# Block-sorted attention and a squared-ReLU feed-forward in one kernel: fewer fp32 heads of q on SyncE, an earlier gate for the first x^T transposes, a new order of the first head pairs

## Chip, core and metric

One core of a Trainium2 chip runs the whole program. The metric is the time of one execution in microseconds (us), the median of several runs. Engine names as in the profile: PE is TensorE's matmuls, PEld its weight loads, DVE VectorE, ACT ScalarE, POOL GpSimd, SP SyncE.

## What is computed

Attention over sorted blocks, then a feed-forward on its output. Batch 4, 8 heads, 768 positions of 64 elements, 8 blocks of 96 positions; the feed-forward takes 3072 tokens of 512 through 2048 hidden units.

```
P = sort_net                                  # [4, 8, 8, 8]
for _ in range(5):                            # Sinkhorn
    P = exp(P - max(P)); P /= sum(P, -1); P /= sum(P, -2)
k_s = einsum('bhij,bhjcd->bhicd', P, k_blocks)
v_s = einsum('bhij,bhjcd->bhicd', P, v_blocks)
o   = softmax(q_b @ k_s^T / sqrt(64)) @ v_s   # block by block
x   = o.transpose(0, 2, 1, 3).reshape(3072, 512)
out = relu(x @ w_in) ** 2 @ w_out             # fp32 [3072, 512]
```

## The kernel before

**Who sets the order.** The kernel does not issue instructions as it meets them. It adds operations to a `Plan`, each with an engine, a cost and what it depends on; `Plan.run` then writes out one fixed order for each engine. PE has two lists there, attention and feed-forward. A table `DUES` gives each attention step of the second half of batch 0 and of batches 1 to 3 a due place, counted in feed-forward chunks, and an attention step goes first when it is due and ready. The first half of batch 0 follows a string `FIRST` instead: K and V sort the block rows of a head pair (L620), S is scores and exponential (L691, L711), T turns the sorted V (L740), A is the product with V and its normalisation (L882, L892, L893), X turns the attention output into x^T (L941), F is a first piece of the up-projection (L968). A capital letter lets ACT copy out of PSUM, a small one DVE; the prime picks the PSUM buffer. The planner's costs are fixed numbers in the code; on the chip every engine works through its list in order.

**Opening.** SP loads `sort_net` and then q of heads 0 to 3 of batch 0 in fp32 into space of `xT` that is needed only later (`q32`, L313). POOL's queue casts while it loads (L324): q of heads 4 to 7 in two halves of 64 partitions, K and V of batch 0 in head pairs, four parts of `w_in`, four parts of `w_out`, and then batch 1: V, V, K, q, K, q, in halves of four heads. ACT and DVE do five Sinkhorn rounds (exponential L459, normalisations L402 to L406), and between the exponentials ACT casts q32 to bf16 (`cast`, L469) and copies the q transposes (L570) out of PSUM (L248). When the sorting matrix is ready (`p_ij`, L417), PE spreads it over the partitions (`p_spread`, L481) and DVE and POOL build the block weights `w_all` (L493).

Filler matmuls on `ones` (`fill`, L431) keep PE at work in the gaps that the plan foresees before the feed-forward starts; they are written into PE's list like everything else. In front of them stand trial instructions whose results nothing uses: four fp32 matmuls (L444), a product with a running sum and a reciprocal on DVE (L436 to L440), and an exponential with a scale from memory on ACT (L449).

**Rest.** From about 23 us on PE alternates between the second half of batch 0 and later batches' attention, and the feed-forward in units of 384 tokens: 64 up matmuls (L1010, ReLU on ACT L1018, square on DVE L1021), then 48 down matmuls (L1040). The second-half sorts of K and V are L656.

For batch 1 and later, sorted V (`vn`, L776) goes through DRAM to change its layout: SP writes `v_way` (L800), waits, and reads `vblk` (L806), which the product L882 needs. q of batch 1's first two pairs is transposed on PE (L570), the other pairs' K and q by the DMA crossbar.

x^T of the second half of batch 0 comes for its first three head pairs from crossbar transposes on SP (L917). The first of them is held back by a small copy on POOL, the gate (L923), that reads the third part of `w_out`, so that the transposes do not start before that part has landed. It is put in the plan where the first such transpose is made, and stands behind all loads of batch 1.

Of the kernel before, what the change touches and what calls it, by code (L numbers as in the profile page):

```python
# [18 lines left out]


DUES = {
    (0, "K"): (-232.0, -238.5, -413.0, -404.5),
    (0, "S"): (-204.0, -204.5, -355.5, -296.0),
    (0, "T"): (-231.5, -163.5, -378.0, -266.0),
    (0, "A"): (-198.0, -109.5, -291.0, -100.5),
    (0, "X"): (-51.5, -27.5, -263.5, -74.5),
    (0, "W"): (-288.5,),
    (1, "V"): (-107.5, -57.0),
    (1, "Q"): (-50.0,),
    (1, "N"): (None, -39.5),  # L30
    (1, "Z"): (None, None, 1.0, 47.5),
    (1, "S"): (-40.5, -15.5, 11.5, 49.5),
    (1, "A"): (-27.5, 2.5, 12.5, 51.5),
    (1, "X"): (22.0, 6.0, 42.5, 54.5),
    (2, "L"): (45.5,),
    (2, "N"): (70.5, 75.5),
    (2, "V"): (73.0, 79.0),
    (2, "Z"): (79.5, 85.0, 93.5, 93.0),
    (2, "S"): (80.0, 85.5, 99.5, 97.0),
    (2, "A"): (80.0, 87.5, 101.0, 98.5),  # L40
    (2, "X"): (89.5, 99.0, 125.0, 130.0),
    (3, "L"): (130.5,),
    (3, "N"): (130.5, 138.5),
    (3, "V"): (132.0, 143.0),
    (3, "Z"): (142.5, 143.0, 153.0, 145.0),
    (3, "S"): (148.0, 148.5, 161.0, 157.0),
    (3, "A"): (148.0, 156.5, 162.5, 157.5),
    (3, "X"): (155.5, 165.0, 169.0, 183.5),
}

FIRST = ("K0 v0 k1' S0 t0' v1 K2' k3 S1 A0 T1' V2' v3 S2 A1 T2' t3' S3 x0' A2 X1 F0 F1 A3 X2 F3 "
         "F4 x3 F6 F7")


class Op:
# [127 lines left out]
def kernel(  # L185
# [115 lines left out]
    for n in range(4):  # L301
# [5 lines left out]
    w_in_bf = const.tile([128, KC, d_ff], BF16)  # L307
    w_out_bf = const.tile([128, NT, d_model], BF16)
    xT = const.tile([128, KC, n_tok], BF16)
    q32 = [xT[:, 1 + g, 2 * S:].bitcast(FP32).rearrange("p (h x) -> p h x", h=2)  # L310
           for g in range(2)]
    for g in range(2):
        nc.sync.dma_start(out=q32[g], in_=q_r[0, :, 2 * g:2 * g + 2, :])  # L313
    w_all = const.tile([128, H + HP, NB, C0], BF16)
    w_t = const.tile([128, NH // 4, 4, NB], BF16)
    qkv = {}
# [35 lines left out]

    first = plan.add("DMA", 4.55, lambda e: None)
    landed["last"] = first
    load(0, 0, HP, HP, slice(0, 64))
    load(0, 0, HP, HP, slice(64, 128))
    id_op = plan.add("POOL", 0.4, lambda e: make_identity(nc, ident, nomemset=True))
    mask = const.tile([128, C0], BF16)
    mask_t = const.tile([128, 4], BF16)
# [21 lines left out]
    def loads_after(deps):  # L381
        for g in range(4):
            if g == 1:
                landed["last"] = plan.add("DMA", 0.4, lambda e: None, [landed["last"]])
            t = slice(NT // 4 * g, NT // 4 * (g + 1))
            dma(("w_out", g), 1.05, lambda t=t: (w_out_bf[:, t, :], w_out_r[:, t, :]), deps)
        for t, g in ((2, 0), (2, 1), (1, 0), (0, 0), (1, 1), (0, 1)):
            load(1, t, HP * g, HP, deps=deps)
            if t == 2 and g == 1:
                landed["last"] = plan.add("DMA", 1.5, lambda e: None, [landed["last"]])  # L390
# [36 lines left out]
    def fill(us, slot):  # L427
# [4 lines left out]
                out=p2[slot][:, 0, 0:128 * r].rearrange("p (r x) -> p r x", r=r), lhsT=ones,  # L432
                rhs=ones[:, None, :].to_broadcast([128, r, 128]), start=True, stop=True)

    t32 = xT[:, 3, 2 * S:].bitcast(FP32)
    nc.vector.memset(t32[:, 0:128], 1.0)  # L436
    nc.vector.scalar_tensor_tensor(
        out=t32[:, 128:136], in0=t32[:, 0:8], scalar=1.0, in1=t32[:, 8:16],
        op0=ALU.mult, op1=ALU.mult, accum_out=t32[:, 136:137])
    nc.vector.reciprocal(out=t32[:, 137:138], in_=t32[:, 136:137])  # L440

    def warm(e):
        for n in (8, 16):
            nc.tensor.matmul(out=p2[1][:, 0, 16 * n:17 * n], lhsT=t32[:, 0:128],  # L444
                             rhs=t32[:, 0:n], start=True, stop=True)
        fill(2.4, 0)

    def try_exp(e):
        nc.scalar.activation(out=t32[:, 140:148], in_=p2[1][:, 0, 128:136], func=AF.Exp,  # L449
                             scale=t32[:, 137:138])  # L450


    plan.add("PE", 4.3, warm, [plan.add("DVE", 1.1, lambda e: None)])
# [4 lines left out]
    for it in range(5):  # L458
        step = plan.add("ACT", 0.26, lambda e: nc.scalar.activation(  # L459
            out=p_sb, in_=p_sb, func=AF.Exp), [step])  # L460
        exps.append(step)
        if it == 0:
            plan.add("ACT", 0.4, try_exp, [step])
        if it == 1:
            plan.add("ACT", 0.6, make_sel, [step, id_op])
        if it in (1, 2):
            def cast(e, g=it - 1):
                alloc_qkv(0)
                nc.scalar.copy(out=qkv[0][0][:, 2 * g:2 * g + 2, :], in_=q32[g])  # L469

            casts.append(plan.add("ACT", 0.8, cast, [step, plan.add(
                "WAY", 2.6 + 0.9 * it, lambda e: None, tail=2.6 + 0.9 * it)]))
        step = plan.add("DVE", 0.66, lambda e: sink_norm(e, 0), [step])
        step = plan.add("DVE", 0.47 if it == 4 else 0.72, lambda e, it=it: sink_norm(e, 1, it == 4), [step])

# [81 lines left out]
    def s_q(b, hp, p0, p1, due=0, after=None, eng=AD):  # L557

        n = p1 - p0
        t = {}  # L560

        def mm(e):
            qb = qkv[b][0]
            if b == 0:
                t["p"] = psf.tile([128, NA, n], BF16, tag="pf", name="qtp")
            else:
                t["p"] = ps1.tile([128, NA, n], BF16, tag="p1", name="qtp")
            for a in range(NA):
                for h in range(2):
                    nc.tensor.transpose(  # L570
                        out=t["p"][64 * h:64 * (h + 1), a, :],
                        in_=qb[p0:p1, 2 * hp + h, D * a:D * (a + 1)],
                        identity=ident[p0:p1, p0:p1])
            if p0 == 0:
                tiles["qT", b, hp] = att.tile(
                    [128, NA, 128], BF16, tag="qT", name="qT", bufs=4)

        def ev(e):
            qT, src = tiles["qT", b, hp].rearrange("p a x -> p (a x)"), t["p"]
            if b == 0:  # L580
                copy(e, qT.rearrange("p (i c a) -> p i c a", a=NA, c=C0)
                     [:, p0 // C0:p1 // C0, :, :], src.rearrange("p a (i c) -> p i c a", c=C0))
            else:
                copy(e, qT.rearrange("p (i a c) -> p i a c", a=NA, c=C0)
                     [:, p0 // C0:p1 // C0, :, :], src.rearrange("p a (i c) -> p i a c", c=C0))

        if b == 0:
            dep = casts[hp] if hp < HP // 2 else landed[b, 0, HP, p0]
        else:
            dep = landed[b, 0, HP * (2 * hp // HP), 0]  # L590
        ring = rf if b == 0 else r1
        s1, old = ring.take()
        if p0 == 0:
            qTs[b, hp], oldq = rqT.take()
        else:
            oldq = []
        pe = plan.add("PE", 0.04 + 0.0023 * n, mm, [dep, id_op] + old, due, mode="col")
        readers[b].append(pe)
        op = one_of(eng, cost_b(NA * n), ev, [pe, after] + oldq)
        ring.use(s1, pe, op)  # L600
        rqT.use(qTs[b, hp], op)
        return op
# [309 lines left out]
    def s_xt(u, due=0, eng=AD, own=True):  # L912
        early = u.b == 0 and u.halves == (1,) and u.hp < HP - 1
        if early or u.b > 1 or u.b == 1 and u.hp < HP - 1:
            def turn(e):
                t0 = S * u.b + BLK * u.i0
                nc.sync.dma_start_transpose(  # L917
                    out=xT[:, u.hp, t0:t0 + BLK * u.ni].rearrange("p (n q) -> p n q", q=BLK),
                    in_=u.ao.rearrange("p n e d -> p (n e d)"))

            if early and "gate" not in holds:
                def gate(e):
                    nc.gpsimd.tensor_copy(out=xT[0:1, 0:HP - 1, HS:HS + 1],  # L923
                                          in_=w_out_bf[0:1, 3 * NT // 4 - HP + 1:3 * NT // 4, 0:1])

                holds["gate"] = plan.add("POOL", 0.1, gate, [landed["w_out", 2]])
            sp = plan.add("SP", 1.4, turn, u.norms + [holds["gate"]] * early)
            op = plan.add("WAY", 6.0 if early else 1.3, lambda e: None, [sp], tail=3.8 if early else None)
            rao.use(u.nao, op)
            for hf in u.halves:  # L930
                x_done[u.b, u.hp, hf] = op
            return
# [46 lines left out]
    def put(key, t, n, dst, pe):  # L979

        st = {}
        so, old = rob.take()

        def cp(e):
            st["ob"] = ffn.tile([128, d_model], FP32, tag="ob", name="ob", bufs=4)
            copy(e, st["ob"][:, 0:n], t[key][:, 0:n])

        op = plan.add(AD, cost_f(n), cp, [pe] + old)
        sp = plan.add("SP", 0.55, lambda e: nc.sync.dma_start(out=dst, in_=st["ob"][:, 0:n]), [op])
        rob.use(so, plan.add("WAY", 1.5, lambda e: None, [sp], tail=0.9))  # L990
        return op

    def ffn_unit(g):
# [224 lines left out]
```

## Time and profile before

| | before |
|---|---|
| median of 3 runs | 219.79 us (219.42 to 220.04) |
| profiled execution | 219.84 us, span 218.1 us |
| PE busy | 209.6 us, 96% of the span |
| ACT, DVE, POOL busy | 121.9, 111.0, 28.3 us |
| DMA moved | 31.92 MB, mean 146 GB/s |
| granted TensorE clock, mean | 1.00 |

How to read the profile: a chain line gives start, length and what the time was spent on, followed back from the last instruction. A timeline line gives start, length, engine, line of the kernel, operation, out<-in and count. A wait line gives engine, what waited, what it waited for, us in total, times, and the longest. A queue line gives packets, MB, and the packets' time as a share of 16 DMA engines; q0 is the queue that POOL feeds, q1 SP's. "L882" is line 882 of the kernel it belongs to; the changed kernel is 18 lines shorter, so the same statement has a smaller number there.

### The profile page before, as it was taken

How to read it: one execution, taken by the hardware profiler on the slowest of the kernel's cores; microseconds unless marked ns; L12 is line 12 of the kernel's file. 1: busy time of each engine (PE TensorE's matmuls, PEld its weight loads, DVE VectorE, ACT ScalarE, POOL GpSimd, SP SyncE). 2: the span in 40 equal slices, each digit the busy share in tenths (PEclk: the TensorE clock that was granted, in tenths of full speed). 3: DMA queues.
4: the chain of work that ended last, by engine and by line, in shares of the span. 5: the costliest groups of instructions: out<-in, count | busy, mean ns of one | idle time of the engine just before them, and what ended most of it. 6: DMA issues, size and time to landing. Idle time of an engine off the chain costs nothing.

```text
span 218.1 us, 5074 instructions
## 1 busy us (share of the span) xinstructions
PE 209.6 (96%) x2024; PEld 116.3 (53%) x2041; DVE 111.0 (51%) x303; ACT 121.9 (56%) x250; POOL 28.3 (13%) x53
## 2 busy tenths in 40 slices
PE   6989999999899999999999999999999999999993
PEld 3457666446554555445665465445655455456552
DVE  6668586335696336653876045617685154015300
ACT  5767778228674457645784177327874375237421
POOL 7985221000000700000000420000000000000000
PEclk9999999999999999999999999999999999999999
DMA  6999999999986699299952699598985310120012
GB/s 152 199 189 207 207 206 212 181 152 278 259 164 59 142 203 227 57 170 252 185 171 52 134 182 221 108 196 185 153 203 116 88 45 3 48 96 0 3 57 89
DMA packets 47864, 31.92 MB, mean 146 GB/s; under 512 B 27296, under 2 KB 42912, under 8 KB 47840
## 3 DMA queue, kind: packets, MB, share of 16 engines
q0 software_dynamic: 12224, 13.24, 37.6%
q1 hardware_dynamic: 35616, 18.35, 37.6%
q8 instruction: 16, 0.26, 0.5%
q14 instruction: 8, 0.07, 0.1%
HBM read 29.70 MB, written 8.72 MB: 176 GB/s over the span
## 4 chain that ended last, share of the span: by engine, by line
PE 78%; DMA 11%; POOL 3%; DVE 3%; issue 1%; ACT 1%; POOLq 0%; DVEq 0%; SPq 0%
PE hp L1010 34%; PE op L1040 33%; DMA v_way<-vn 6%; DMA kb<-in_k_dram 3%; PE p L882 3%; PE p L691 3%; DMA vblk<-v_way 2%; PE op L1068 2%; PE p L776 1%; DVE ao L893 1%; POOL vb L324 1%; POOL kb L324 1%; PE p L656 1%; ACT h L1018 1%; DVE h L1021 1%
## 5 line engine op out<-in xcount | busy, mean ns | idle before, releaser
L1010 PE MATMUL hp<-xT,w_in_bf 128*128 128x384 bf16 x506 | 87.8, 326 | 0.0
L1040 PE MATMUL op<-w_out_bf,h 128*128 128x512 bf16 x351 | 83.4, 379 | 1.1 <-issue 0.3
L1018 ACT ACTIVATE h<-hp 128x384 bf16<-128x384 f32 x128 | 61.7, 495 | 19.5 <-PE hp L1010 16.5
L1021 DVE TENSOR_TENSOR h<-h 128x384 bf16<-128x384 bf16 x128 | 43.7, 355 | 49.1 <-ACT h L1018 48.6
L1010 PEld LDWEIGHTS <-w_in_bf 128*128 128x128 bf16 x506 | 47.5, 98 | 31.4 <-issue 0.5
L1040 PEld LDWEIGHTS <-h 128*128 128x128 bf16 x368 | 34.0, 98 | 38.4 <-issue 1.4
L248 ACT COPY ob<-op 128x512 f32<-128x512 f32 (+2 forms) x24 | 13.6, 568 | 47.1 <-PE op L1040 44.7
L720 ACT ACTIVATE et<-p 96x384 bf16<-96x384 f32 x48 | 19.7, 488 | 7.4 <-PE p L691 7.4
L893 DVE TENSOR_TENSOR ao<-p,rec 96x512 bf16<-96x512 f32 x32 | 22.0, 686 | 1.1
L882 PEld LDWEIGHTS <-et 96*128 96x128 bf16 x256 | 11.4, 97 | 5.3 <-DMA vblk<-v_way 0.9
L892 DVE RECIPROCAL rec<-p 96x8 f32<-96x8 f32 x32 | 6.4, 201 | 14.9 <-PE p L882 14.6
L1157 POOL COPY held<-xT 1x3 bf16<-1x3 bf16 (+1 forms) x2 | 0.4, 186 | 83.1 <-DMA xT<-ao 83.1
L882 PE MATMUL p<-vblk,et 96*128 96x65 bf16 x192 | 9.3, 193 | 0.6 <-DMA vblk<-v_way 0.6
L431 PE MATMUL p<-ones 128*128 128x512 bf16 (+1 forms) x29 | 9.2, 436 | 0.0
L691 PEld LDWEIGHTS <-kvT 64*128 64x128 bf16 x256 | 6.2, 94 | 5.5 <-issue 3.1
L250 DVE CAST vn<-p 128x768 bf16<-128x768 f32 x6 | 5.7, 958 | 6.1 <-PE p L776 6.0
L250 DVE CAST kn<-p 128x768 bf16<-128x768 f32 x5 | 4.8, 958 | 7.6 <-PE p L776 7.5
L836 DVE COPY kvT<-kx 128x768 bf16<-128x768 bf16 x10 | 8.5, 848 | 0.1
L248 ACT CAST vn<-p 128x768 bf16<-128x768 f32 x6 | 4.8, 801 | 5.4 <-PE p L776 5.4
L711 ACT ACTIVATE et<-p 96x768 bf16<-96x768 f32 x8 | 6.3, 807 | 1.4 <-PE p L691 1.4
L324 POOL DMA_DIRECT2D kb<-in_k_dram x10 | 6.4, 637 | 4.4 <-DMA w_in_bf<-in_moe_w_in_dram 2.0
L324 POOL DMA_DIRECT2D vb<-in_v_dram x10 | 6.2, 620 | 3.5 <-DMA w_in_bf<-in_moe_w_in_dram 3.5
(89 smaller groups left out, 120.1 us busy)
## 6 DMA issues: line engine op xcount, KB each, us to landing
out_dram<-ob SPq DMA_DIRECT2D x23, 256.0 KB, 3.1
v_way<-vn SPq DMA_DIRECT2D x6, 396.0 KB, 4.6
vblk<-v_way SPq DMA_DIRECT2D x6, 396.0 KB, 4.2
vb<-in_v_dram POOLq DMA_DIRECT2D x6, 384.0 KB, 11.9
kb<-in_k_dram POOLq DMA_DIRECT2D x6, 384.0 KB, 10.5
qb<-in_q_dram POOLq DMA_DIRECT2D x6, 384.0 KB, 13.3
w_in_bf<-in_moe_w_in_dram POOLq DMA_DIRECT2D x4, 512.0 KB, 12.5
w_out_bf<-in_moe_w_out_dram POOLq DMA_DIRECT2D x4, 512.0 KB, 17.0
```

The source lines that it names most:

```text
L248: nc.scalar.copy(out=out, in_=in_)
L250: nc.vector.tensor_copy(out=out, in_=in_)
L324: nc.gpsimd.dma_start(out=dst, in_=src)
L431: nc.tensor.matmul(out=p2[slot][:, 0, 0:128 * r].rearrange("p (r x) -> p r x", r=r), lhsT=ones, rhs=ones[:, None, :].to_broadcast([128, r, ...
L691: nc.tensor.matmul(out=scp[:, h, BLK * n:BLK * (n + 1)], lhsT=u.ksT[64 * h:64 * (h + 1), HS * hf + BLK * n:HS * hf + BLK * n + 128], rhs=( ...
L720: nc.scalar.activation(out=et[:, h, 0:HS].rearrange("p (n c a) -> p n c a", c=C0, a=NA), in_=st["p"][0:96, h, 0:HS].rearrange("p (n a c) - ...
L882: nc.tensor.matmul(out=oup[:, h, 66 * n:66 * n + D + 1], lhsT=et_r[u.et[hf]][:, h, BLK * n:BLK * n + 128], rhs=(u.vs[:, NQ * hf + n, h, 0: ...
L893: nc.vector.tensor_tensor(out=u.ao[:, n0:n0 + NQ, :, :].rearrange("p n e d -> p e n d"), in0=ov[:, :, :, 0:D], in1=rec[:, :, :, None].to_b ...
L1010: nc.tensor.matmul(out=t["hp", nt][:, 0:HS], lhsT=w_in_bf[:, kc, 128 * nt:128 * (nt + 1)], rhs=xT[:, kc, t0:t0 + HS], start=(kc == 0), sto ...
L1018: nc.scalar.activation(out=t["h1", nt], in_=t["hp", nt][:, 0:HS], func=AF.Relu)
L1021: nc.vector.tensor_tensor(out=t["h2"][:, nt, :], in0=t["h1", nt], in1=t["h1", nt], op=ALU.mult)
L1040: nc.tensor.matmul(out=t["op", mt], lhsT=t["h2"][:, nt, 128 * mt:128 * (mt + 1)], rhs=w_out_bf[:, nt, :], start=(nt == 0), stop=(nt == NT ...
```

## The change

- SP loads q of heads 0 and 1 in fp32 (one transfer, one cast on ACT, now ahead of `make_sel`), POOL loads heads 2 to 7.
- The gate reads the second part of `w_out` instead of the third, and stands on POOL in front of the last load of batch 1, which depends on it.
- The trial instructions are left out.
- `FIRST` is another order: the first two pairs are sorted together, all six F pieces come after the third X.
- `DUES` has other numbers throughout, and two costs in the plan change. This moves instructions in every engine's list; the counts of attention and feed-forward instructions stay.

```diff
 DUES = {
...
-    (1, "V"): (-107.5, -57.0),
-    (1, "Q"): (-50.0,),
-    (1, "N"): (None, -39.5),
+    (1, "V"): (-103.0, -81.0),
+    (1, "Q"): (-67.0,),
+    (1, "N"): (None, -30.0),
...
-    (1, "A"): (-27.5, 2.5, 12.5, 51.5),
-    (1, "X"): (22.0, 6.0, 42.5, 54.5),
+    (1, "A"): (-7.0, 5.5, 20.0, 52.0),
+    (1, "X"): (44.0, 40.5, 23.0, 54.5),
...
-FIRST = ("K0 v0 k1' S0 t0' v1 K2' k3 S1 A0 T1' V2' v3 S2 A1 T2' t3' S3 x0' A2 X1 F0 F1 A3 X2 F3 "
-         "F4 x3 F6 F7")
+FIRST = ("K0' v0 K1 v1 S0 t0' S1 t1' A0 K2 V2' A1 K3 S2 t2' v3 S3 x1 A2 T3' x0' A3 X2 F0 F1 F3 "
+         "F4 F6 F7 x3")
...
-    q32 = [xT[:, 1 + g, 2 * S:].bitcast(FP32).rearrange("p (h x) -> p h x", h=2)
-           for g in range(2)]
-    for g in range(2):
-        nc.sync.dma_start(out=q32[g], in_=q_r[0, :, 2 * g:2 * g + 2, :])
+    q32 = xT[:, 1, 2 * S:].bitcast(FP32).rearrange("p (h x) -> p h x", h=2)
+    nc.sync.dma_start(out=q32, in_=q_r[0, :, 0:2, :])
...
-    load(0, 0, HP, HP, slice(0, 64))
-    load(0, 0, HP, HP, slice(64, 128))
+    load(0, 0, 2, H - 2, slice(0, 64))
+    load(0, 0, 2, H - 2, slice(64, 128))
...
+        def gate(e):
+            nc.gpsimd.tensor_copy(out=xT[0:1, 0:HP - 1, HS:HS + 1],
+                                  in_=w_out_bf[0:1, NT // 2 - HP + 1:NT // 2, 0:1])
+
         for t, g in ((2, 0), (2, 1), (1, 0), (0, 0), (1, 1), (0, 1)):
+            if t == 0 and g == 1:
+                holds["gate"] = plan.add("POOL", 0.1, gate, [landed["w_out", 1]])
+                deps = [holds["gate"]]
             load(1, t, HP * g, HP, deps=deps)
...
-    t32 = xT[:, 3, 2 * S:].bitcast(FP32)
-    nc.vector.memset(t32[:, 0:128], 1.0)
-    nc.vector.scalar_tensor_tensor(
-        out=t32[:, 128:136], in0=t32[:, 0:8], scalar=1.0, in1=t32[:, 8:16],
-        op0=ALU.mult, op1=ALU.mult, accum_out=t32[:, 136:137])
-    nc.vector.reciprocal(out=t32[:, 137:138], in_=t32[:, 136:137])
-
     def warm(e):
-        for n in (8, 16):
-            nc.tensor.matmul(out=p2[1][:, 0, 16 * n:17 * n], lhsT=t32[:, 0:128],
-                             rhs=t32[:, 0:n], start=True, stop=True)
         fill(2.4, 0)
-
-    def try_exp(e):
-        nc.scalar.activation(out=t32[:, 140:148], in_=p2[1][:, 0, 128:136], func=AF.Exp,
-                             scale=t32[:, 137:138])
...
-        if it == 0:
-            plan.add("ACT", 0.4, try_exp, [step])
         if it == 1:
+            def cast(e):
+                alloc_qkv(0)
+                nc.scalar.copy(out=qkv[0][0][:, 0:2, :], in_=q32)
+
+            casts.append(plan.add("ACT", 0.83, cast, [step, plan.add(
+                "WAY", 4.3, lambda e: None, tail=4.3)]))
             plan.add("ACT", 0.6, make_sel, [step, id_op])
-        if it in (1, 2):
-            def cast(e, g=it - 1):
-                alloc_qkv(0)
-                nc.scalar.copy(out=qkv[0][0][:, 2 * g:2 * g + 2, :], in_=q32[g])
-
-            casts.append(plan.add("ACT", 0.8, cast, [step, plan.add(
-                "WAY", 2.6 + 0.9 * it, lambda e: None, tail=2.6 + 0.9 * it)]))
...
-            dep = casts[hp] if hp < HP // 2 else landed[b, 0, HP, p0]
+            dep = casts[hp] if hp < 1 else landed[b, 0, 2, p0]
...
-            if early and "gate" not in holds:
-                def gate(e):
-                    nc.gpsimd.tensor_copy(out=xT[0:1, 0:HP - 1, HS:HS + 1],
-                                          in_=w_out_bf[0:1, 3 * NT // 4 - HP + 1:3 * NT // 4, 0:1])
-
-                holds["gate"] = plan.add("POOL", 0.1, gate, [landed["w_out", 2]])
             sp = plan.add("SP", 1.4, turn, u.norms + [holds["gate"]] * early)
-            op = plan.add("WAY", 6.0 if early else 1.3, lambda e: None, [sp], tail=3.8 if early else None)
+            op = plan.add("WAY", 6.4 if early else 1.3, lambda e: None, [sp], tail=3.4 if early else None)
...
-        rob.use(so, plan.add("WAY", 1.5, lambda e: None, [sp], tail=0.9))
+        rob.use(so, plan.add("WAY", 1.5, lambda e: None, [sp], tail=0.6))
```

## The prediction

> **What bounds the kernel now.** I read the page first, then the chain of waits in order of time, then the timeline and the DMA view of the stretches where the chain is not TensorE work.
>
> ```profile
> span 218.1 us, 5074 instructions
> ...
> PE 209.6 (96%) x2024; PEld 116.3 (53%) x2041; DVE 111.0 (51%) x303; ACT 121.9 (56%) x250; POOL 28.3 (13%) x53
> ...
> PE   6989999999899999999999999999999999999993
> ```
>
> PE is full from the fifth slice on. What can move is when the feed-forward work begins (about 23 us), the few holes after it, and the amount of PE work. The profiled execution took 219.84 us for a span of 218.1, and lies 0.05 above the median of 219.79. The chain over the opening:
>
> ```profile
> 8.86 7.56 DMA kb<-in_k_dram
> ...
> 16.95 0.56 DVE kvT L250
> ...
> 21.74 0.70 DVE ao L893
> ...
> 22.48 0.34 PE xtp L941 x4
> ```
>
> The K rows of the last head pair land at 16.42; behind them DVE runs without a break through one copy and the four softmax normalisations. The rest of the opening is decided earlier, in the timeline:
>
> ```profile
> 11.56 0.20 DVE L417 STREAM_TRANSPOSE p_ij<-pf 32x32 bf16<-32x32 bf16 x1
> ...
> 11.95 0.38 PE L570 MATMUL qtp<-ident,qb 64*64 64x64 bf16 x12
> ...
> 12.26 0.61 PE L431 MATMUL p<-ones 128*128 128x512 bf16 x2
> ...
> 12.80 0.36 PE L481 MATMUL pt_ps<-p_ij,xT 32*128 32x32 bf16 x8
> ```
>
> The sorting matrix (p_ij, first half) is there at 11.76, but PE spreads it (L481) only at 12.8: it is still working through q transposes and filler matmuls ordered before it. Third, the only sizeable PE wait after 24 us, and the chain behind it:
>
> ```profile
> PE p L882 <- DMA vblk<-v_way: 0.6, 1, 0.6
> ```
>
> ```profile
> 41.67 12.68 DMA v_way<-vn
> ...
> 54.41 4.67 DMA vblk<-v_way
> ...
> 59.13 0.67 PE p L882 x16
> ```
>
> Sorted V of batch 1 goes out to DRAM and back, and takes 17.4 us because the queues are full. The DMA view of 42 to 45 us shows how they share: the two queues pass equal numbers of packets.
>
> ```profile
> q0 software_dynamic: 579, 0.43, 92.2%
> q1 hardware_dynamic: 586, 0.13, 38.0%
> ```
>
> **The opening, part by part.** *Trial instructions.* DVE loses 0.69 us (0.17+0.28+0.08+0.16), ACT 0.27, PE 1.04, all before 3.3 us. DVE's first reduction at 2.60 waits for the exponential that ends at 2.57, so this is worth nothing there; without that cover it could be worth up to the 0.69. On PE the filler starts when its ones are set (1.01) instead of at 2.80: ten at the 0.43 spacing of their weight loads end at 5.4, not 7.1.
>
> *q through POOL.* By the windows, 3 to 4 us moved 251 packets (201 of SP's, 50 of POOL's), 7 to 15 us 1979 packets, 247 per us. A row of a head is one packet either way, so 1024 q packets take as long in either queue, and K and V behind them should land as now. Issue plus landing time now: K 8.5, 11.2, 14.0, 16.4; V 10.3, 13.0, 15.65, 17.5; first w_in part 20.0. The q halves land at 6.05 and 7.5 and I keep that. POOL still issues two q transfers (0.76 and 0.63 now), so nothing on POOL moves. A packet could cost 0 to 20% more in POOL's queue (4 us for the 1024 now): 256 moved ones, 0 to 0.2 us; I take 0, the 247-per-us row.
>
> *ACT* gets one cast (0.83) instead of two. The Sinkhorn exponentials now start at 2.31, 4.14, 5.90, 7.82 and 9.84. The first free period is 5.90-4.14 = 1.76; the fourth and fifth are held by q copies on ACT. After the change copies of pair 0 come between 6.1 and 6.6, those of pairs 1 to 3 (q at 6.05, three transposes, 3 x 0.41) end near 9.2, so the exponentials fall at 7.66 and 9.42 and p_ij at 9.42+1.92 = 11.34. PE's ordered list before L481 holds, from the q of 6.05 on, 12 wide fillers, 5 half ones and 7 sets of q transposes: 12 x 0.23 + 5 x 0.12 + 7 x 0.26 = 5.2, so it ends near 11.2. L481 starts near 11.4 instead of 12.8: **1.37 earlier**.
>
> A rule speaks against that. The Trainium skill ("TensorE: Matmul & The Clock Gate", Part 1) says PE leaves half clock only after about 3.4 us of sustained work seen through a free-running window. Here the weight loads of the fillers go from 0.43 to 0.33 apart after 6.17, some 4.3 us after PE's first work at 1.92; by that row the clock rises near 5.5 in the new kernel. By the rule a broken filler train could be seen cold until about 8, an estimate from that page; L481 would then lose most of its lead.
>
> *The new order* FIRST. I walked it with the durations of the profile (K, V copies 0.48 on ACT and 0.54 on DVE, exponential 0.81, normalisation 0.20+0.69, xT copy 0.36) from L481 at 11.4. Now loads decide: V of pair 1 at 13.0, V of pair 2 at 15.65 (PE stands before the second softmax product for it), K of pair 3 at 16.5, V of pair 3 at 17.6 with its copy on DVE to 18.55, its transpose on PE to 19.35, copied by ACT to 20.0, last product to 20.45, normalised by 21.4, six pieces of the first up-projection in front of the last x^T transpose, that at 21.75, and the second-half sorts at 22.05. They start at 23.08 now: **-1.03**. The same walk from 12.8 gives 22.7: -0.35. More than L481's lead of 1.37 can't come. I take 1.03, as both holds of ACT are seen in the exponentials' starts.
>
> **After the opening.** The ordered lists hold the same 506 up and 400 down matmuls, and the same attention work, in both kernels.
>
> *Score matmuls in smaller groups.* A group of 16 costs 0.45, the feed-forward group after it 0.11 more than its bare 0.1625 each (1.41 against 1.30 for eight). Two groups of 8 cost 2 x (0.28+0.11). Two pairs more are split: 2 x (0.78-0.56) = **+0.44**.
>
> *The wait for vblk.* 98 up matmuls stood before that product since 24 us, now 114: 16 x 0.1625 = 2.6 us more cover. PE comes at 58.56-1.03+2.6 = 60.1. The bytes before vblk are the same, so it lands near 59.1; the 0.56 goes (**-0.56**) with 1 us to spare. If vblk came 1.6 later the wait would be back.
>
> *The gate.* It waits for the second w_out part (32.8) instead of the third (35.4). Three transposes, 1.3 us of SP each and 11.7 at most to landing now, are issued from 33.0 on, and the third, at 35.6, lands by 47.3; the second feed-forward unit, which now puts eight up matmuls before q of batch 1, needs them at 48.1, so 0.8 later would begin to cost. On POOL only the last q load stands behind the gate, and it was issued at 33.1 anyway. But SP's queue empties sooner, and its next transfers then take slots from POOL's loads before q of batch 1: one output tile, 256 KB, and part of v_way. q lands at 49.0 now, and PE takes it at 49.15, with nothing to spare; after the change PE asks for it at 49.15-1.03+1.35 = 49.5. Price: from 50 to 51 us, with v_way under way, 332 packets moved, and 162 of POOL's pass where 247 would: 0.34 us lost to 170 v_way packets, and all its 768 cost 1.6; an output tile is 256 KB at the 323 GB/s of 3 to 4 us, 0.8. With half of v_way in front of q it lands at 49.0+0.8+0.8 = 50.6. In the other direction, 46 to 48 us moved 106 GB/s against 195 at 42 to 45, a hole of 0.9 us with transposes in flight, which need not recur: 49.7. So the wait is 0.2 to 1.1, and 0 if no v_way packet is in front; I take **+0.40**, nearer the lower end, as the transposes are over by then.
>
> *Third w_out part and later.* The fourth part lands at 38.0 and is needed at 39.2; transposes beside it can delay it by at most 0.9. Covered by 0.3.
>
> Sum: -1.03+0.44-0.56+0.40 = **-0.75**; 219.84-0.75 = 219.09 for a profiled execution, 219.0 for the median.
>
> **Rivals.** (1) *The opening hardly moves*: PE's fillers stay cold or q lands over 1 us later, and L481 stays near 12.8. For it: PE's list is in order and filler times were wrong by 1 us before. Against: fillers start 1.7 us earlier. -0.35 in place of -1.03: 219.7. (2) *Batch 1's q comes late.* All of v_way and the output tile pass in front of it and the hole recurs: 49.0+0.8+1.6 = 51.4, a wait of 1.9 and a sum of -1.03+0.44-0.56+1.9 = +0.75: 220.5. It makes the kernel slower than before once q lands after 50.65, and slower by over 0.3% after 51.3. For it: the equal packet counts of the two queues; against: v_way is ready only near 44 and waits behind the transposes. (3) *No q wait at all*: 218.6.
>
> **How the numbers follow.** Forecast 0.50 (218.6 to 219.4), rival (1) 0.20 (219.4 to 220.2), rival (2) 0.17 (220.0 to 221.2), rival (3) 0.13 (218.1 to 218.7). 0.3% is 0.66 us, about what a measurement of this kernel can tell from no change: faster lies below 219.13, slower above 220.45. Faster: 0.33 of the forecast and all of (3), 0.46. Slower: three quarters of (2), 0.13. Same: 0.41. The range 218.2 to 220.6 leaves out the ends of (2) and (3). The forecast's own range is 218.6 to 219.4.
>
> **What would show it.** Right: exponentials near 7.7 and 9.4, L469 (the old L481) near 11.4, second-half sorts near 22.05, no PE wait for vblk, PE waiting 0 to 1.1 us for qb near 49.5. The steps are wrong if L469 stays after 12.5, if K or V of batch 0 land over 0.5 us later, or if PE waits for anything else after 24 us. The forecast is wrong if q of batch 1 lands after 51.

## The result, and the profile after

The changed kernel takes 218.87 us (median of 20 executions, 218.15 to 221.49) where the kernel before took 219.61 beside it (20 executions): a ratio of 0.9962, 95% interval 0.9949 to 0.9975. A second series of 12 gave 218.81 against 219.61, 0.9959 (0.9937 to 0.9980). That is 0.8 us, against 0.75 forecast; but the steps behind the forecast did not all hold. The profiled execution took 218.50 us with a span of 216.7, so it lies 0.4 below the median. A few executions run disturbed, among them the 221.49 above and the profiled one of the kernel with four heads in the held order; the ratios leave these out.

The page of the changed kernel: span, engines, PE's slices.

```profile
span 216.7 us, 5072 instructions
...
PE 209.8 (97%) x2020; PEld 115.6 (53%) x2036; DVE 110.3 (51%) x300; ACT 120.1 (55%) x247; POOL 28.6 (13%) x53
...
PE   7998999989999999999999999999999999999994
```

PE has as much work as before (209.8 against 209.6). The span is shorter mainly because PE gets to the second-half sorts and the feed-forward behind them earlier. The chain over the opening (start, length, what):

```profile
8.95 7.52 DMA kb<-in_k_dram
...
16.51 0.38 PE tp L608 x12
...
19.04 0.59 ACT qz L248
...
21.52 0.88 PE p L644 x48
```

K of the last pair lands at 16.47, as before (16.42), but behind it there is no longer DVE's row of normalisations: the chain goes over PE and one ACT copy to the second-half sorts. In the timeline of the same stretch (changed kernel, then the kernel before):

```profile
5.40 0.38 PE L558 MATMUL qtp<-ident,qb 64*64 64x64 bf16 x12 [0.20 <-ACT qb L456]
...
11.42 0.20 DVE L422 STREAM_TRANSPOSE p_ij<-pf 32x32 bf16<-32x32 bf16 x1
...
11.68 0.57 PE L469 MATMUL pt_ps<-p_ij,xT 32*128 32x32 bf16 x8
...
21.45 0.38 PE L644 MATMUL p<-w_all,kb 128*64 128x64 bf16 x12
```

```profile
23.08 0.38 PE L656 MATMUL p<-w_all,kb 128*64 128x64 bf16 x12
```

The spread (L469, before L481) now follows p_ij (there at 11.62) at once and comes 1.1 us earlier; the second-half sorts come at 21.45, 1.63 earlier than 23.08. PE's waits of any size after 24 us have become another one, and the chain behind it:

```profile
PE hp L992 <- DMA xT<-ao: 0.5, 1, 0.5
```

```profile
35.85 12.16 DMA xT<-ao
...
48.05 1.48 PE hp L992 x8
49.53 0.46 PE qtp L558 x12
...
60.17 0.50 PE p L870 x16
```

The wait for vblk (0.6) is gone: it lands at 59.0, PE comes at 60.0. In its place the eight early up matmuls wait for the third early x^T transpose, which is issued at 35.85 and lands at 48.01. The q of batch 1 that was forecast late landed at 48.5, before PE asks for it at 49.46. From 42 to 45 us the queues share as before, packet for packet:

```profile
q0 software_dynamic: 575, 0.43, 91.2%
q1 hardware_dynamic: 578, 0.14, 36.5%
```

### The profile page after: what moved, and what is told of

Same layout as the page of the kernel before. It is cut to its first block, busy times and chain, and to the rows that moved or that the text cites. A ratio compares the mean times of both kernels' runs of the same rounds, so it can differ in the third digit from the quotient of the medians.

```text
span 216.7 us, 5072 instructions
## 1 busy us (share of the span) xinstructions
PE 209.8 (97%) x2020; PEld 115.6 (53%) x2036; DVE 110.3 (51%) x300; ACT 120.1 (55%) x247; POOL 28.6 (13%) x53
## 4 chain that ended last, share of the span: by engine, by line
PE 83%; DMA 9%; POOL 3%; issue 1%; ACT 1%; DVE 1%; POOLq 0%
PE hp L992 38%; PE op L1022 32%; DMA xT<-ao 6%; PE p L870 4%; DMA kb<-in_k_dram 3%; PE p L679 3%; PE op L1050 2%; PE p L764 1%; POOL kb L322 1%; POOL vb L322 1%; PE p L644 1%; PE vbp L728 1%; ACT h L1000 1%; POOL qb L322 1%; DVE h L1003 1%
## 5 line engine op out<-in xcount | busy, mean ns | idle before, releaser
L992 PEld LDWEIGHTS <-w_in_bf 128*128 128x128 bf16 x506 | 47.3, 98 | 32.4 <-DMA xT<-ao 1.0
L870 PEld LDWEIGHTS <-et 96*128 96x128 bf16 x256 | 11.4, 97 | 5.2 <-issue 0.7
L322 POOL DMA_DIRECT2D qb<-in_q_dram x8 | 6.1, 764 | 2.6 <-DMA w_in_bf<-in_moe_w_in_dram 1.8
## 6 DMA issues: line engine op xcount, KB each, us to landing
vb<-in_v_dram POOLq DMA_DIRECT2D x6, 384.0 KB, 12.2
```

Source lines behind the costliest of these rows:

```text
L322: nc.gpsimd.dma_start(out=dst, in_=src)
L870: nc.tensor.matmul(out=oup[:, h, 66 * n:66 * n + D + 1], lhsT=et_r[u.et[hf]][:, h, BLK * n:BLK * n + 128], rhs=(u.vs[:, NQ * hf + n, h, 0: ...
L992: nc.tensor.matmul(out=t["hp", nt][:, 0:HS], lhsT=w_in_bf[:, kc, 128 * nt:128 * (nt + 1)], rhs=xT[:, kc, t0:t0 + HS], start=(kc == 0), sto ...
```

## The experiments

Theory A is the prediction's: the gain is made in the opening, by the order of first pairs and the earlier spread together; the wait for vblk goes, and part of the gain is given back to a wait near 48 us and to split score pairs. The rivals name one part as the whole cause: the shorter fp32 load (C), the trial instructions or the spread's lead (C2, D), the due times (F), or say that a wait isn't where A puts it (B).

**The gate, one part later and one part earlier.** Every engine's order stays.

```diff
-    in_=w_out_bf[0:1, NT // 2 - HP + 1:NT // 2, 0:1])            # second part
+    in_=w_out_bf[0:1, 3 * NT // 4 - HP + 1:3 * NT // 4, 0:1])    # third (first kernel)
+    in_=w_out_bf[0:1, NT // 4 - HP + 1:NT // 4, 0:1])            # first (second kernel)
```

> The changed kernel, with its gate reading the third w_out part instead of the second; the order of every engine stays as it is. Theory A (the early x^T transposes land a fixed 9 to 12 us after their issue, and the 0.5 us wait of the eight early up matmuls L992 is set by the gate): they are issued near 35.6 instead of 33.2, the third lands near 50, as it did in the kernel before (issued at 38.3, 11.7 to landing), the wait grows from 0.5 to 2.0 to 2.5 and the time from 218.9 to 220.4 to 220.9. Rival B (they land when POOL's queue of loads runs low, whenever they were issued): third landing 48 to 48.5, wait under 0.9, 218.9 to 219.3.

> The changed kernel, with its gate reading the first w_out part, so that the early x^T transposes are issued near 30.9 instead of 33.2. Theory A (issue sets landing): the third lands near 46, the eight early up matmuls wait for nothing, PE asks for q of batch 1 at 49.0 and finds it (48.5): 0.5 us less, 218.4. The price may be the fourth w_out part, which lands at 37.7 and is asked for near 38.3: up to 0.5 us of a wait there would eat the gain. Rival B (POOL's backlog sets landing): third still near 48, 218.9.

Third part: 221.79 us, ratio 1.0103 (1.0073 to 1.0132). Its wait and the chain behind it:

```profile
PE hp L992 <- DMA xT<-ao: 2.7, 1, 2.7
```

```profile
38.68 12.29 DMA xT<-ao
```

Issued 2.8 us later, the third transpose lands 3.0 us later and the wait grows from 0.5 to 2.7: issue sets landing (A), and B falls. The time lies above A's 220.4 to 220.9; PE also waited 0.8 for w_in in the opening of the profiled execution. First part: 221.52, ratio 1.0098 (1.0063 to 1.0133), where A expected a gain. The transposes no longer hold anything up, though the third, issued 2.1 us earlier, lands only 1.0 earlier (46.99; A had 46). Its waits show the price:

```profile
PE op L1022 <- DMA w_out_bf<-in_moe_w_out_dram: 2.3, 1, 2.3
```

The fourth w_out part, in flight together with the earlier transposes, lands at 40.7; in the two traces of the changed kernel it lands at 37.9 and 38.5. A had put that price at 0.5 at most. The second part is the best of the three places: one part earlier or later takes 2.7 to 2.9 us more than the changed kernel, over three times what the whole change brings.

**Four fp32 heads again,** in two forms: with the planner told of it (it then fits a new order), and with the order held.

```diff
-    nc.sync.dma_start(out=q32, in_=q_r[0, :, 0:2, :])
+    for g in range(2):
+        nc.sync.dma_start(out=q32[g], in_=q_r[0, :, 2 * g:2 * g + 2, :])
```

> The changed kernel, with four fp32 heads of q on SyncE in two loads and two casts on ACT, as in the kernel before. Theory A (the opening's gain comes from the order of first pairs and from the sorting matrix being spread earlier, and the second cast holds one exponential by 0.1 to 0.4 us only): spread L469 at 11.7 to 12.1, K and V of the first pairs up to 1 us earlier, second-half sorts at 21.3 to 21.8, 218.7 to 219.1. Rival C (the shorter fp32 load is what brings the opening forward): spread near 12.5 to 12.8 and 219.3 to 219.6.

> The changed kernel, with four fp32 heads of q on SyncE in two loads and two casts on ACT, but, unlike the run with four heads above, with every engine's order as in the changed kernel: the planner is told nothing of it. Theory A (the shorter fp32 load brings nothing; what the earlier run lost was its new order, in which PE waits 1.6 us for V of batch 1): spread L469 at 11.6 to 12.1, no wait for V of batch 1, 218.7 to 219.1. Rival C (the second fp32 load and its cast do cost): 219.4 or more.

With a new order: 220.16, ratio 1.0017 (0.9996 to 1.0038). Its opening loses nothing: spread at 11.83, second-half sorts at 21.34, first down product at 35.64 (changed kernel 35.68). It loses later, in a wait that only its own order has:

```profile
PE p L767 <- DMA vb<-in_v_dram: 1.6, 1, 1.6
```

So the shorter fp32 load is not what brings the opening forward (C falls). With the order held: 221.13, ratio 1.0051 (1.0022 to 1.0080), a miss. The edit put the second cast right behind the first, in front of the third exponential, and there it waits. The timeline of its profiled execution, ACT and PE, and PE's stretches of 3.4 us (busy time of PE, PEld, DVE, ACT and POOL with the count of instructions, then PEclk, DMA share, GB/s):

```profile
4.29 0.81 ACT L460 CAST qb<-xT 128x768 bf16<-128x768 f32 x1
...
7.33 0.83 ACT L460 CAST qb<-xT 128x768 bf16<-128x768 f32 x1 [2.22 <-DMA xT<-in_q_dram]
...
8.58 0.25 ACT L453 ACTIVATE p_sb<-p_sb 32x64 f32<-32x64 f32 x1
```

```profile
4.30:7.70 3.40, 1.48 (x17) 0.48 (x15) 1.27 (x6) 1.18 (x3) 3.17 (x9) 1.00 1.22 246
7.80:11.10 3.30, 2.89 (x41) 1.72 (x42) 1.68 (x9) 2.15 (x7) 3.30 (x6) 0.50 1.21 179
```

ACT stands 2.2 us for the second transfer, with the third exponential behind it (8.58 where the changed kernel has 6.17); PE runs dry and is then granted half the clock until 21.4. In nine of the other twelve executions the mean granted clock was 0.992; the two with 1.00 took 219.45 and 219.76. This is no clean price of four heads: the order was not quite held, and one trace shows what a second cast in front of an exponential can cost when its load is late. Where those nine lost their clock was not seen.

**The trial instructions,** put back into the changed kernel and taken out of the kernel before; nothing else moves in the lists.

```diff
     def warm(e):
+        for n in (8, 16):
+            nc.tensor.matmul(out=p2[1][:, 0, 16 * n:17 * n], lhsT=t32[:, 0:128], ...)
         fill(2.4, 0)
```

> The changed kernel, with the trial instructions of the kernel before put back (a memset, a multiply-accumulate, a reciprocal on DVE, two narrow fp32 matmuls ahead of PE's fillers, one exponential on ACT). Theory A (they cost little): PE's fillers start 1 to 1.7 us later and have less time to warm, the spread L469 comes 0 to 0.5 later than 11.68, second-half sorts 0 to 0.3 later, as K and V landings decide there: 218.9 to 219.2. Rival C2 (taking them out is what brings the opening forward): L469 near 12.8, second-half sorts near 23.0, 219.7 or more.

> The kernel before, without its trial instructions and nothing else changed; every engine's order is the same otherwise. Putting the trial instructions into the changed kernel moved its spread L469 from 11.68 to 12.72 and its time to 219.68. Theory A (lead and order work together: in the old order the opening is held by K of pair 3 at 16.4 and by the chain on DVE behind it, so an earlier spread brings little): spread L481 near 11.7, second-half sorts L656 at 22.8 to 23.1, 219.3 to 219.6. Rival D (the lead of the spread is the whole gain, whatever the order): sorts near 22.0, 218.7 to 218.9.

Put back: 219.68, ratio 1.0008 (0.9996 to 1.0021): the whole gain is gone. That is C2's time, but not its way there. The fillers start at 2.79 instead of 1.06, the spread comes at 12.72, yet the second-half sorts lose only 0.39:

```profile
21.84 0.38 PE L660 MATMUL p<-w_all,kb 128*64 128x64 bf16 x12
...
28.07 0.22 PE L660 MATMUL p<-w_all,vb 128*64 128x64 bf16 x1 [0.56 <-issue]
```

The other line is a hole of 0.56 inside a group of sorts that nothing in the profile ends; it is not in the changed kernel, whose list is the same there. With it the first down product is 1.22 late (36.90). Some 0.7 of that is made good by 50 us, most of it because PE then finds the third x^T transpose landed, and 0.5 is lost again in a wait for vblk at 113.9 that the changed kernel does not have. Whether the hole comes in each execution, and from what, stays open. Taken out of the kernel before: 219.47, ratio 0.9994 (0.9970 to 1.0017), no gain, as A has it. D's 218.7 to 218.9 touches the low end of the interval (218.75) and is unlikely, not excluded; the kernel with the old order below speaks against it. (Its profiled execution is not like the others: PE waited 1.4 us for K of pair 3 and 0.8 for q, and its clock fell; so it tests neither the spread nor the sorts that A gave. See the end.)

**The order of first pairs,** alone in the kernel before, and undone in the changed kernel. The planner fits the later steps anew in both.

```diff
 # into the kernel before; the other kernel has the reverse
-FIRST = ("K0 v0 k1' S0 t0' v1 K2' k3 S1 A0 T1' V2' v3 S2 A1 T2' t3' S3 x0' A2 X1 F0 F1 A3 X2 F3 ...
+FIRST = ("K0' v0 K1 v1 S0 t0' S1 t1' A0 K2 V2' A1 K3 S2 t2' v3 S3 x1 A2 T3' x0' A3 X2 F0 F1 F3 ...
```

> The kernel before, with the new order of first pairs alone; trial instructions, four fp32 heads, the gate on the third w_out part and the due times stay. The planner fits the steps after the opening anew, which may move the time by 0.5 either way. Theory A (order alone, from a spread at 12.8: 0.35 of the gain): second-half sorts at 22.5 to 22.8, down products 0.3 to 0.6 earlier than 37.43, 219.0 to 219.4 before that fitting. Rival D (the lead of the spread is the whole gain): sorts at 23.0, 219.6.

> The changed kernel, with the old order of first pairs; everything else as changed, the steps after the opening fitted anew by the planner (0.5 either way). Theory A (order and lead work together): spread near 11.7, second-half sorts back at 22.7 to 23.0 and 219.6 to 220.2. Rival D (the lead of the spread is the whole gain): sorts at 21.5 to 22.0 and 218.7 to 219.1.

New order alone: 222.57, ratio 1.0129 (1.0092 to 1.0165). Undone: 220.56, ratio 1.0040 (1.0013 to 1.0068). Both times lie above what A gave, by steps behind the opening; the openings are what tells. The profiled executions, one for each row, in which PE was warm by the spread and nothing cooled it in the opening, by order:

| order | spread at | second-half sorts at | kernel |
|---|---|---|---|
| old | 12.80 | 23.08 | before |
| old | 12.05 | 23.04 | order undone |
| new | 13.80 | 22.93 | new order alone (fourth exponential 0.7 later than in the kernel before, the fifth 1.0) |
| new | 12.72 | 21.84 | trial instructions put back |
| new | 12.41 | 21.91 | old due times (below) |
| new | 12.02 | 21.53 | gate on the first part |
| new | 11.84 | 21.34 | four heads, new order |
| new | 11.82 | 22.22 | gate on the third part (PE waits 0.8 for w_in) |
| new | 11.68 | 21.45 | changed (11.68 and 21.50 in the second series) |
| new | 11.51 | 21.42 | 12 fillers (below) |

In the old order 0.75 us of lead bring 0.04; in the new one 1.04 bring 0.39. At about the same spread (12.80 and 12.72) old and new order lie 23.08-21.84 = 1.24 apart; these two kernels also differ in the q loads, the gate and the due times. The changed kernel and the one with the order undone, alike in those, lie 1.59 apart, of which the later spread (0.37) can explain 0.37 at most. The new order alone shows no such gain: its spread came 1.0 later than in the kernel before, and its sorts miss A's 22.5 to 22.8. The chain of the kernel with the order undone shows why the lead is lost there: DVE, from 16.8 on, behind K of pair 3 (landed at 16.23), as in the kernel before.

```profile
16.76 0.56 DVE kvT L250
...
21.70 0.70 DVE ao L881
...
22.44 0.34 PE xtp L923 x4
```

**The due times,** set back in the changed kernel.

```diff
 DUES = {
-    (0, "K"): (-262.5, -244.5, -414.0, -379.0),
+    (0, "K"): (-232.0, -238.5, -413.0, -404.5),
...
```

> The changed kernel with the old due times; opening, gate and loads as changed. Theory A (the gain lies in the opening, and later steps give back what their fitting leaves): spread at 11.7, first down product at 35.5 to 36.0, then 0.3 to 1.5 us lost to waits for transposed x or q of batch 1, which the old due times were not fitted to: 218.9 to 220.2. Rival F (the due times bring the gain): 219.6 or more with the down product no earlier than 37.0. Rival G (the new due times only cost, by two more split pairs at 0.22 each): 218.2 to 218.6.

All rows of the table are set back. 221.38, ratio 1.0088 (1.0056 to 1.0119), above all three. The opening is kept: first down product at 36.26 although PE waited 0.9 for q early on, and the sixth output tile is stored at 76.97, as in the changed kernel (76.98; 78.64 in the kernel before). Then two waits come that neither kernel has:

```profile
125.78 10.24 PE L992 MATMUL hp<-xT,w_in_bf 128*128 128x384 bf16 x62 [0.97 <-DMA xT<-ao]
...
174.85 10.23 PE L992 MATMUL hp<-xT,w_in_bf 128*128 128x384 bf16 x62 [1.00 <-DMA xT<-ao]
```

The kernel with the new order alone, which also has the old due times, has the same two (1.9 in all). So the due times bring no gain by themselves (F falls), but without them the new order loses 2 us again in front of the feed-forward units of batches 2 and 3. G falls too: the old ones are not cheaper.

**Filler matmuls at the head.** The trial instructions put back with 6 fillers, and the changed kernel with 12, beside the changed kernel as it is (10).

```diff
-        fill(2.4, 0)
+        fill(1.44, 0)    # with the trial instructions: 6 fillers
+        fill(2.9, 0)     # changed kernel: 12 fillers
```

> The changed kernel with the trial instructions put back, as in the run above, but with 6 of the 10 filler matmuls at the head of PE's list instead of 10: the trial instructions start the fillers 1.74 us later, and four fillers at 0.43 take 1.72. Theory A (what the trial instructions cost is their place in PE's list, in front of the spread): the first q transposes near 5.4 to 5.6, the spread L469 back at 11.6 to 11.8, first down product at 35.5 to 36.0, 218.7 to 219.1. Rival E (they cost something else, on DVE, ACT or by a colder clock): spread 12.2 or later, 219.5 to 219.8.

> The changed kernel with two more filler matmuls at the head of PE's list (12 instead of 10), which close PE's 0.2 us gap before the first q transposes. Theory A (PE reaches the spread 0.49 us before the sorting matrix is there, so that there is some slack): the q transposes start near 6.0 instead of 5.4, the spread at 11.7 to 12.0, 218.8 to 219.2; the granted clock stays at 0.997 or more in every run, as PE doesn't run dry when q comes late. Rival (no slack): spread at 12.3, 219.3.

> The changed kernel as it is, beside the three others of this call: 218.6 to 219.1. Theory A has a weak point in PE's idle time before the first q transposes (0.2 in its profile, 0.6 to 0.8 in three experiments whose loads came later): in some runs the granted clock may fall under 0.995, and those runs take 220 or more. If none does, the 0.2 is short enough.

Six fillers: 219.82, ratio 0.9991 (0.9967 to 1.0016), in two groups: three executions of 218.2 to 218.7 and nine of 219.2 to 220.5. The profiled one is of the second, and its seven fillers in the middle show why (the changed kernel's beneath):

```profile
8.23 2.96 PE L436 MATMUL p<-ones 128*128 128x512 bf16 x7
```

```profile
7.15 1.58 PE L436 MATMUL p<-ones 128*128 128x512 bf16 x7
```

At 0.42 each instead of 0.23 PE still runs cold after 11 us, and the spread comes at 14.29. The first q transposes do come at 5.45, as A has them, but the fillers are needed to warm PE: E holds for this execution. That the three fast ones are those where PE warmed in time is an inference; there is no trace of them. Twelve fillers: 218.79, ratio 0.9968 (0.9944 to 0.9993), spread at 11.51; the same as the changed kernel's 218.81 in the second series. Two more fillers cost nothing, but the slack of 0.49 that A names isn't there: the weight loads of the spread stand idle 0.49 before it, and 0.42 of that stands there in the kernel before too, where p_ij has long been waiting. In the profile with 12 fillers full clock came at 4.07 instead of 4.75, so that they end at 5.30, hardly later than the ten (5.20). No execution of either was under 0.998 in granted clock. This mean leaves out a cold start (the six-filler profile has 1.00 with full clock only from 11.77); that the 0.2 us gap was short enough rests on the two traces of the changed kernel, both at full clock from 4.75, and on the times of its second series, all under 220. No version beats the changed kernel.

## Why the prediction was right, and where not

Against the medians the sum was right to 0.1 us, in part by luck: its terms err both ways. From the profiled pair, end of PE's work, in us:

| step | forecast | measured |
|---|---|---|
| opening, to the second-half sorts | -1.03 | -1.63 |
| wait for vblk | -0.56 | -0.56 |
| wait near 48 to 49 us | +0.40 (q of batch 1) | +0.49 (third x^T transpose) |
| batch 2 with its split score pairs (77 to 125 us, as a whole) | +0.44 | +0.62 |
| rest, not placed | 0 | +0.05 |
| end of PE's work | -0.75 | -1.03 |

*One pair is one draw.* The first profiled execution is 1.34 shorter than that of before; 0.3 of this lies behind the last output's landing, where the kernel does no work. The second profiled execution of the changed kernel ends PE's work only 0.37 earlier than that of before, with a wait of 0.8 for the transposes; the medians say 0.8.

*The opening* is the term that was mis-sized. The spread was forecast at 11.4 and came at 11.68: the first exponential started at 2.54 instead of 2.31, with the last gaps at 1.76 as forecast, so p_ij came at 11.62 instead of 11.34. PE's list, forecast to reach the spread near 11.2, reached it near 11.6 too, by the spacing behind its last fillers; in the traces of the two moved gates and the old due times p_ij is there 0.4 to 1.0 before the spread, and the list alone sets it. From there the walk was too long. V of pair 3 and its DVE copy came as walked (18.54), but its transpose on PE was charged to 19.35 and was done at 19.00, so that ACT's copy (19.63), the last product (20.08) and the last x^T transpose (21.17, forecast 21.75) came 0.4 to 0.6 sooner. The split inside the term was wrong as well: the walk gave the order alone 0.35 and the lead 0.68 more; the traces give 1.24 and 0.39. Rival (1), a spread still near 12.8 for 219.7, is what the run with the trial instructions has, and it took 219.68; but 0.39 of that loss lies where the rival put 0.68, and the rest after it.

*K and V of batch 0* did not land as before: K of the first two pairs at 9.7 and 12.2 instead of 8.5 and 11.2, as more q stands before them in POOL's queue: its second half lands at 8.73, where the prediction kept 7.5. With four heads on SyncE again K lands at 8.6 and 11.1. This was named as a sign of a wrong step, and it was one; it cost nothing here, because the spread at 11.68 comes later than the first of them, the second is needed at 13.0, and V of pair 3 lands at 17.4 as before (17.5).

*The gate* was bounded by "lands by 47.3, needed at 48.1". It landed 0.7 later (issued 0.25 later, 12.16 in flight instead of at most 11.7) and was needed 0.5 earlier (47.56), as the opening had gained 0.6 more. The 0.8 of cover and 0.5 more were used up. *The wait for q* (+0.40) that was charged in its place didn't come: q landed at 48.5, earlier than the 49.0 of before, so the packets that were counted against it did not delay it. A wait of like size in another place made the sum right. Rival (2) fails on q. Rival (3), no wait for q, was right on it, and its 218.6 is missed only because PE waits for the transposes instead. The first gate experiment shows that 2.8 us of later issue would have made the kernel slower by the way of the transposes instead.

*The fourth w_out part* was called covered by 0.3. In the two traces of the changed kernel it was; in the profile with 12 fillers, gate and order as changed, it landed at 39.4 and PE waited 0.9 for it.

*The clock rule* that spoke against the lead (half clock until about 3.4 us of sustained work: the Trainium skill, "TensorE: Matmul & The Clock Gate", Part 1) was weighed rightly for this kernel: full clock was granted from 4.75 us on, 3.7 after the first filler, against 6.40 before, and the filler train broken from 5.20 to 5.40 did not lose it. That a longer dry stretch can lose the clock is seen in two other traces (last section).

*Trial instructions* were priced at 0 for DVE and as filler time on PE. Putting them back costs 0.8 us in the median. In the profiled execution 0.39 of it is seen in the sorts; the rest is the hole of 0.56, whose cause is open, and a later wait for vblk.

## What to carry to other kernels

An earlier start is worth what the order behind it can use: here 0.75 us of lead brought the second-half sorts 0.04 in the old order, and between a kernel with the old and one with the new order, at about the same spread, they lie 1.24 apart, so walk the chain behind a step before pricing its lead. A gain in the opening is not yet a gain at the end: that kernel with the new order and the old spread took 219.68 in all, no less than the kernel before. A list order, the transfers that it waits for and the priorities fitted to it are one design; taking one of the three back, or making one of them alone, made the kernel 1.3 to 3.2 us slower (than the changed kernel, or than the kernel before), where all together bring 0.8. A transfer that is gated to stay out of the way has to be priced on both sides, by what it delays and by who waits for it.

## What the runs showed of the hardware

*The clock is granted in pieces of 3.41 us.* In the traces' clock records every stretch between the first and the last change is a multiple of it: 3.413, 13.653 (4 times), 211.63 (62 times). The Trainium skill ("TensorE: Matmul & The Clock Gate", Part 1) says so of a free-running window of 3413 ns, and the runs agree. PE's busy share alone does not tell which piece loses the clock. In the kernel before without trial instructions two stretches run, in the columns given above,

```profile
15.80:19.20 3.40, 2.06 (x66) 1.65 (x67) 1.63 (x5) 1.82 (x5) 2.99 (x5) 1.00 1.25 206
19.30:22.60 3.30, 3.30 (x42) 2.66 (x40) 2.50 (x7) 2.37 (x4) 0.54 (x1) 0.50 1.25 209
```

PE was busy for 61% of one piece (most of a wait of 1.40 for K in it) and got half the clock in the next. In the kernel with the gate on the first part a piece with 46% (most of its wait of 2.3 in it) was followed by full clock, while 44% (1.48 of 3.40) in the kernel with four heads in the held order, shown above, was followed by half:

```profile
38.93:42.34 3.41, 1.57 (x8) 0.74 (x8) 0.00 (x0) 0.51 (x1) 0.00 (x0) 1.00 1.15 184
42.35:45.75 3.40, 3.40 (x35) 1.41 (x34) 0.92 (x1) 0.92 (x3) 0.00 (x0) 1.00 1.48 141
```

Nor does a full share bring it back at once: in that last profile PE was busy throughout from 11.2 to 17.9, and half the clock stayed until 21.4. What else decides stays open. One lost piece is worth up to 3.41 x 0.5 = 1.7 us and makes the mean granted clock 0.992. Means of 0.976 to 0.992 came in 2 of 6 and 3 of 7 executions of the kernels with the gate moved, and in none of 32 of the changed kernel. The profiled executions of the moved gates have one PE wait of 2.3 and 2.7 us and kept full clock through it; the longest waits in the changed kernel's, after the start, are 0.5 and 0.8. Where the others lost the clock was not traced. So a wait of 1.4 us can cost a second time, and a longer one need not.

*Crossbar transposes behind a full POOL queue* took 7 to 13 us from issue to landing. They seem to hold the queue's own loads up: issued 2.1 us earlier, in one trace, they go with a fourth w_out part 2.2 to 2.9 us later than in the two traces of the changed kernel.
